# The last block of each chain behind the second product, transposes one block product later, last additions by halves

## The chip, the cores and the metric

One NeuronCore of a Trainium2 chip runs the whole program in one launch. The metric is the device time of one execution in microseconds (us). Engines by their short names: PE (matrix products, with PEld for its weight loads), DVE (vector), ACT (scalar), POOL (GpSimd), SP (which issues the DMAs). Each engine works through its own queue in order and waits on semaphores for the others.

## The reference

Local attention over 2304 tokens gives rows of 512 numbers; a first feed-forward block with ELU follows, then a mixture of eight experts whose weights `P` come from a softmax that is normalised by rows and columns eight times:

```python
for e in range(E):                       # 8 experts, F = 1024
    h = np.maximum(x @ w1[e], 0.0)       # x: 2304 x 512
    ye = h @ w2[e]
    out += P[:, e:e + 1] * ye
```

Everything is float32. The change touches only this last loop.

## The kernel before

Attention and the first block end at about 540 us, the softmax and five experts of the first 768 tokens at about 860 us. From there to the end runs the part that is changed. It takes the tokens in three groups of 768 (group 0 still lacks experts 5 to 7; groups 1 and 2 need all eight) and replaces each product of 2x2 blocks by seven block products (the scheme of Strassen and Winograd). Each float32 operand is held as a high and a low half, so one block product of 384 columns is 3 matmuls for each of two chunks of 128.

The work is cut into **periods**, one for each group, expert and half of the hidden units (6, 16 and 16 of them), and a period into seven **slots** `j`. A slot `s` issues, in program order:

- two block products of the first layer, by `l1` (6 matmuls each, into PSUM tiles `la` or `lb`). They belong to two **chains** `p` = 0 and 1. A chain takes its seven products `pi` in the order 1, 2, 6, 7, 5, 3, 4; chain 0 ends in slot 3, chain 1 in slot 6, each with product 4 into `lb`.
- one block product of the second layer, by `l2`, of the period eight slots earlier (`LAG`). For groups 1 and 2 that is `l2_flip`: 12 matmuls into a tile of two PSUM banks, `oa` and `ob` in turn, then one DVE addition of 768 columns into the sum `acc`. Column half `c` of the result lies in bank `c` of the tile.

Behind each `l1` stand operations that turn its PSUM result into the hidden blocks. ACT keeps copies (`a`, `u`, `v`, L1091); DVE adds them (`c`, L1085 and L1111), scales by `P` (L1081), and forms the sums of the scheme (`s`, L1095, with L1118 in front). Product 4 adds three: `c` <- `lb`, `u`; the scaling; a last `s`. Then `put` queues, in the list `after`, the split of each hidden block into halves: ACT copies the high half (L1044), DVE (L1049) or POOL (L1053) forms the low one. The list is emptied behind the next `l1` that isn't product 4.

At the end of a group the additions of the last four block products of `l2` (`done`, out of order 1, 7, 6, 4, 5, 2, 3) complete the four quarters of the result. Each is then added as two halves of 384 columns, both issued behind all 12 matmuls, and queues two `out_unit`s: three PE transposes into a tile `ot` of the ring `lb` (two buffers, shared with products 2, 7, 5 and 4 of the chains), an ACT copy to `ost`, and a DMA to the output. They are issued behind the `l2` of the next slot.

The order in each queue is the order in which this code calls the operations; no scheduler moves anything. Weights come by DMA, 12 tiles of `w1f` and 7 of `w2f` ahead.

Of the kernel before, what the change touches and what calls it, by code (L numbers as in the profile page):

```python
# [11 lines left out]
AF = mybir.ActivationFunctionType  # L12
ALU = mybir.AluOpType
# [5 lines left out]
def kernel(  # L19
# [14 lines left out]
    nc = tc.nc  # L34
# [645 lines left out]
    rest = others[N1 + N3:]  # L680
    for u in range(2 * KP):
        hs = [(4 * u + i, (4 * u + i) % 8) for i in range(4)]
# [176 lines left out]
    TH = 384  # L859
    NG2 = NT // (2 * TH)  # L860
# [81 lines left out]
    NPD = len(periods)  # L942
# [93 lines left out]

    chains = {}
    H = {}
    after = []

    def hid(key, slot, src, relu):
        h = P2["hp"].tile([P, 2, TH], R32, tag=f"h{slot}", bufs=3, name=f"h{slot}")
# [15 lines left out]
    def l1(k, n, p, pi):  # L1058
        key = (k, p)
        d = chains.setdefault(key, {})  # L1060
        if pi == 1:
            d["A"] = P2["ps2"].tile([P, 512], F32, tag="la", bufs=2, name="la")
        elif pi in (2, 7):
            d["B" if pi == 2 else "C"] = P2["ps2"].tile([P, 512], F32, tag="lb", bufs=2, name="lb")
        o = d["A" if pi in (1, 6, 5, 3) else "B" if pi == 2 else "C"][:, :TH]
        w, x = w1t.pop(n), xf[SLB[pi]]
        first = pi in (1, 2, 7)
        last = pi in (3, 2, 4)
        for c in range(2):
            for z, (a, b) in enumerate(((0, 0), (0, 1), (1, 0))):  # L1070
                nc.tensor.matmul(  # L1071
                    o, w[:, a, c, :], x[:, b, c, :],
                    start=first and c == 0 and z == 0, stop=last and c == 1 and z == 2,
                    skip_group_check=True,
                )

        g, e, _ = periods[k]

        def scaled(t, i):
            if g:  # L1080
                nc.vector.tensor_tensor(out=t, in0=t, in1=pb[g, e][:, i], op=ALU.mult)  # L1081

        def add(nm, a):
            t = tmp("c", 5, nm)
            nc.vector.tensor_tensor(out=t, in0=o, in1=d[a], op=ALU.add)  # L1085
            scaled(t, 0)
            d[nm] = t

        def keep(nm):
            d[nm] = tmp("a", 5, nm)  # L1090
            nc.scalar.activation(d[nm], o, AF.Copy)  # L1091

        def ssum(nm, a, b, op):
            d[nm] = tmp("s", 6, nm)
            nc.vector.scalar_tensor_tensor(d[nm], d[a], 0.0, d[b], op0=ALU.max, op1=op)  # L1095

        def put(slot, nm, relu):
            after.append(lambda: hid_low(*hid(key, slot, d[nm], relu)))

        if pi == 1:  # L1100
            keep("a")
        elif pi == 2:
            add("c11", "a")
            put(0, "c11", True)
        elif pi == 6:
            keep("u")
        elif pi == 5:
            keep("v")
            c = d["C"][:, :TH]
            t = tmp("c", 5, "c22")  # L1110
            nc.vector.tensor_tensor(out=t, in0=c, in1=d["v"], op=ALU.add)  # L1111
            scaled(t, 1)
            d["c22"] = t
            put(2, "c22", True)
        elif pi == 3:
            d["r21"] = tmp("s", 6, "r21")
            if g:
                nc.vector.scalar_tensor_tensor(  # L1118
                    d["r21"], o, 0.0, pb[g, e][:, 1], op0=ALU.max, op1=ALU.mult
                )  # L1120
            else:
                nc.scalar.activation(d["r21"], o, AF.Relu)
            ssum("s3", "c11", "r21", ALU.subtract)
            ssum("s1", "c22", "r21", ALU.add)
            ssum("s2", "c11", "s1", ALU.subtract)
            put(5, "s3", False)
            put(4, "s2", False)
            put(3, "s1", False)
        elif pi == 4:
            add("c21", "u")  # L1130
            ssum("s4", "c21", "s2", ALU.add)
            put(1, "c21", True)
            put(6, "s4", False)
            del chains[key]


    units = []

    def l2_flip(g, o, w, hs, fresh, i, j, init, done):
        acT = oa[g].rearrange("p a d -> p (a d)").rearrange("p (c t) -> p c t", c=NCC)  # L1140
        o = o.rearrange("p (c n) -> p c n", c=2)[:, :, :TH]
        for c in range(2):
            for p in range(2):
                for z, (a, b) in enumerate(((0, 0), (0, 1), (1, 0))):
                    nc.tensor.matmul(  # L1145
                        o[:, c],
                        w[:, p, b, c * P:(c + 1) * P],
                        hs[p][:, a, :],
                        start=fresh and p == 0 and z == 0,
                        stop=False,  # L1150
                        skip_group_check=True,
                    )
        ts = slice(i * TH, (i + 1) * TH)
        for cs in ((0, 1), (1, 2)) if done else ((0, 2),):
            a = acT[:, 2 * j + cs[0]:2 * j + cs[1], ts]
            src = o[:, cs[0]:cs[1]]
            if init:
                nc.scalar.activation(a, src, AF.Copy)
            else:
                nc.vector.tensor_tensor(out=a, in0=src, in1=a, op=ALU.add)  # L1160
        if done:
            units.append([lambda c=c: out_unit(g, acT, i, 2 * j + c) for c in range(2)])

# [16 lines left out]
    def l2(k, x):  # L1180
        g, e, pp = periods[k]
        pi = out_order[x]
        if x == 0:
            banks.reverse()
            ot["A"] = P2["ps2"].tile([P, 1024], F32, tag=banks[0], bufs=1, name=banks[0])
            if g == 2:
                oa[2] = oa[1]
            elif k and periods[k - 1][0] != g:
                oa[g] = accp.tile([P, 6, DM], F32, tag="acc2", name="acc2")
        if pi in (7, 2):  # L1190
            ot["B"] = P2["ps2"].tile([P, 1024], F32, tag=banks[1], bufs=1, name=banks[1])
        o = ot["A" if pi in (1, 6, 5, 3) else "B"]
        w = w2t.pop(7 * k + x)
        hs = [H.pop(((k, p), SLA[pi])) for p in range(2)]
        fresh = pi in (1, 7, 2)
        i, j, init = {
            1: (0, 0, True), 7: (1, 1, True), 6: (1, 0, True), 4: (1, 0, False),
            5: (1, 1, False), 2: (0, 0, False), 3: (0, 1, True),
        }[pi]
        last = pi in (2, 5, 4, 3)  # L1200
        done = last and e == E - 1 and pp == NP // 2 - 1
        if g:
            l2_flip(g, o, w, hs, fresh, i, j, init and e == 0 and pp == 0, done)
            return
        for c in range(3):
            for p in range(2):
                for z, (a, b) in enumerate(((0, 0), (0, 1), (1, 0))):
                    nc.tensor.matmul(  # L1208
                        o[:, c * HB2:(c + 1) * HB2],
                        hs[p][:, a, c * P:(c + 1) * P],  # L1210
                        w[:, p, b, :],
                        start=fresh and c != 1 and p == 0 and z == 0,
                        stop=False,
                        skip_group_check=True,
                    )
        for c in range(3):
            tt = 3 * i + c
            pe = Pr[:, g * 6 + tt, e:e + 1]
            a = oa[g][:, tt, j * HB2:(j + 1) * HB2]
            src = o[:, c * HB2:(c + 1) * HB2]  # L1220
            if init and e == 0 and pp == 0:
                nc.vector.tensor_scalar(a, src, pe, None, op0=ALU.mult)
            else:
                nc.vector.scalar_tensor_tensor(a, src, pe, a, op0=ALU.mult, op1=ALU.add)
        if done:
            t0 = (2 * g + i) * TH
            nc.sync.dma_start(
                out=out[t0:t0 + TH, j * HB2:(j + 1) * HB2].rearrange("(c p) d -> p c d", p=P),
                in_=oa[g][:, 3 * i:3 * i + 3, j * HB2:(j + 1) * HB2],
            )  # L1230


    with tc.manual_schedule():
# [6 lines left out]
            out=mask[:WIN], in_=mask[:WIN], compare_op=ALU.is_gt, fill=-1.0e9 / scale,  # L1240
# [4 lines left out]
            out=mask[:WIN], in_=mask[:WIN], compare_op=ALU.is_ge, fill=-1.0e9 / scale,  # L1245
# [50 lines left out]
        for m in range(NST + 3):  # L1296
# [58 lines left out]
            out=gw[:, :, E:2 * E], in0=gwr, in1=r(gw[:, :, 0:E]), op=ALU.subtract  # L1355
# [146 lines left out]
        for s in range(NPD * 7 + LAG):  # L1502
            k, j = divmod(s, 7)
            if k < NPD:
                for z, (p, pi) in enumerate(pairs[j]):
# [3 lines left out]
                    for f in fs:  # L1509
                        f()  # L1510
                    w1_load(s * 2 + z + NW1)
            while after and k >= NPD:
                after.pop(0)()
            fs = [f for u in units for f in u]
            units.clear()
            if s == LAG - 3:
                l2(0, 0)
            elif s > LAG:
                l2(*divmod(s - LAG, 7))
            for f in fs:  # L1520
                f()
            while nw2 <= min((s + 1) // 2 if s <= LAG else LAG // 2 + (s - LAG) * 3 // 2, s - LAG + NW2):
                w2_load(nw2)
                nw2 += 1
# [52 lines left out]
```

## Time and profile before

| what | value |
|---|---|
| time of three runs | 1990.64, 1994.05 and 1994.36 us, median 1994.05 |
| the profiled execution | 1989.62 us, of which its span is 1987.8 us |
| PE busy | 1968.5 us, 99% of the span |
| DVE, ACT, POOL busy | 73%, 43%, 37% of the span |
| PE's share of the chain that ended last | 91% (DVE 3%, ACT 2%, DMA 2%) |

PE is busy almost always, so an idle microsecond of PE is nearly a microsecond of the time. A busy share says nothing of who waits for whom; that is read from the waits and from the order of time. Times in the rows are us from the start of the span; a row of the timeline merges equal instructions that follow each other, and its bracket names the idle time before them with what ended it. A row of windows holds a stretch, its length, the busy time of PE, PEld, DVE, ACT and POOL (with the number of instructions), the granted clock of PE as a share of full speed, the share of the DMA engines and GB/s.

### The profile page before, as it was taken

The page shows a single profiled execution, that of the slowest core. Times are in us where ns is not written, and L with a number is a line of the kernel's source. Part 1 is how long each engine was busy: PE and PEld are TensorE (multiplying, and loading weights), DVE is VectorE, ACT ScalarE, POOL GpSimd, SP SyncE. Part 2 cuts the span into 40 slices and gives each one's busy share as a digit, 9 for nine tenths or more (in the row PEclk, how much of TensorE's full clock was granted, in tenths as well). Part 3 has the DMA queues.
Part 4 walks back from the last instruction along what each step waited for, and adds up shares of the span by engine and source line. Part 5 has one row for each costly group of instructions (what it writes and reads, how often), then busy time and mean ns, then how long its engine had stood idle before and what let it go on. Part 6 is the DMA issues. An engine that isn't in the chain of part 4 may idle for free.

```text
span 1987.8 us, 33576 instructions
## 1 busy us (share of the span) xinstructions
PE 1968.5 (99%) x11856; PEld 1826.8 (92%) x11856; DVE 1460.9 (73%) x2526; ACT 848.4 (43%) x1801; POOL 745.2 (37%) x725
## 2 busy tenths in 40 slices
PE   9999999999999999999999999999999999999998
PEld 7778888898878888899999999999998999999998
DVE  6745776767688666566787877887797877787786
ACT  8866455555443444343343333333334333333332
POOL 5423232333265555352262333323253323233232
PEclk9999999999999999999999999999999999999999
DMA  9751254457599999968878888888887888888883
GB/s 215 161 107 40 83 174 154 161 188 270 210 372 371 373 358 367 344 220 270 279 255 294 263 261 252 258 265 259 264 291 240 265 263 262 259 262 260 243 271 113
DMA packets 307718, 487.85 MB, mean 245 GB/s; under 512 B 79888, under 2 KB 162016, under 8 KB 303712
## 3 DMA queue, kind: packets, MB, share of 16 engines
q1 hardware_dynamic: 306288, 485.39, 76.0%
q8 instruction: 95, 1.56, 0.3%
q14 instruction: 71, 0.58, 0.1%
q10 hardware_dynamic: 1264, 0.33, 0.1%
HBM read 354.44 MB, written 126.95 MB: 242 GB/s over the span
## 4 chain that ended last, share of the span: by engine, by line
PE 91%; DVE 3%; ACT 2%; DMA 2%; issue 1%; SPq 0%; ACTq 0%; DVEq 0%
PE la L1071 16%; PE ob L1145 12%; PE oa L1145 11%; PE lb L1071 11%; PE p L879 3%; PE p L880 3%; PE p L881 3%; PE ac L897 3%; PE ac L898 3%; PE ac L899 3%; PE oa L1208 2%; PE ob L1208 2%; PE ac L531 2%; PE ac L532 2%; PE ac L533 2%; PE p L204 2%
## 5 line engine op out<-in xcount | busy, mean ns | idle before, releaser
L1053 POOL TENSOR_TENSOR h<-s,h 128x384 fp32r<-128x384 f32 x304 | 359.5, 1213 | 705.7 <-PE lb L1071 353.5
L1071 PE MATMUL la<-xf,w1f 128*128 128x384 f32 x1824 | 359.6, 335 | 0.7 <-ACT u L1091 0.7
L1071 PEld LDWEIGHTS la<-xf,w1f 128*128 128x128 f32 x1824 | 318.3, 188 | 1.4 <-ACT u L1091 1.3
L1071 PE MATMUL lb<-xf,w1f 128*128 128x384 f32 x1368 | 273.7, 334 | 0.0
L1145 PE MATMUL oa<-h,w2f 128*128 128x384 f32 x1344 | 251.3, 334 | 3.5 <-DVE acc L1160 3.5
L1145 PE MATMUL ob<-h,w2f 128*128 128x384 f32 x1344 | 251.2, 334 | 0.0
L1071 PEld LDWEIGHTS lb<-xf,w1f 128*128 128x128 f32 x1368 | 239.8, 188 | 0.0
L1145 PEld LDWEIGHTS oa<-h,w2f 128*128 128x128 f32 x1344 | 234.4, 188 | 4.2 <-DVE acc L1160 4.2
L1145 PEld LDWEIGHTS ob<-h,w2f 128*128 128x128 f32 x1344 | 234.4, 188 | 0.2
L1044 ACT ACTIVATE h<-s 128x384 fp32r<-128x384 f32 x304 | 146.7, 520 | 165.0 <-DVE s L1095 148.3
L1049 DVE SCALAR_TENSOR_TENSOR h<-c,h 128x384 fp32r<-128x384 f32 x228 | 161.5, 710 | 68.4 <-ACT h L1044 64.5
L718 POOL TENSOR_TENSOR sw<-rw 128x256 f32<-128x256 f32 x110 | 104.6, 951 | 202.9 <-DVE f L748 154.1
L1044 ACT ACTIVATE h<-c 128x384 fp32r<-128x384 f32 x228 | 119.1, 522 | 115.4 <-DVE c L1081 108.0
L1081 DVE TENSOR_TENSOR c<-c,pb 128x384 f32<-128x384 f32 x192 | 133.9, 698 | 6.6
L1160 DVE TENSOR_TENSOR acc<-oa,acc 128x768 f32<-128x768 f32 (+1 forms) x114 | 104.9, 923 | 28.9 <-PE oa L1145 28.9
L1160 DVE TENSOR_TENSOR acc<-ob,acc 128x768 f32<-128x768 f32 (+1 forms) x110 | 101.1, 923 | 28.3 <-PE ob L1145 28.3
L1095 DVE SCALAR_TENSOR_TENSOR s<-c,s 128x384 f32<-128x384 f32 x152 | 110.9, 730 | 13.8 <-DVE s L1095 0.5
L1091 ACT ACTIVATE a<-la 128x384 f32<-128x384 f32 x76 | 37.4, 492 | 191.2 <-PE la L1071 191.2
L246 ACT ACTIVATE hh<-p 128x512 fp32r<-128x512 f32 (+1 forms) x80 | 39.2, 491 | 186.0 <-PE p L881 186.0
L247 DVE SCALAR_TENSOR_TENSOR hl<-p,hh 128x512 fp32r<-128x512 f32 (+1 forms) x80 | 44.3, 556 | 90.1 <-ACT hh L246 90.1
L879 PE MATMUL p<-xh,f 128*128 128x512 f32 (+1 forms) x320 | 108.7, 340 | 0.0
L1091 ACT ACTIVATE v<-la 128x384 f32<-128x384 f32 x76 | 37.3, 491 | 165.9 <-PE la L1071 165.8
(172 smaller groups left out, 4077.6 us busy)
## 6 DMA issues: line engine op xcount, KB each, us to landing
w1f<-wdi SPq DMA_DIRECT2D x532, 256.0 KB, 4.0
w2f<-wdo SPq DMA_DIRECT2D x266, 512.0 KB, 4.3
wdo<-f SPq DMA_DIRECT2D x28, 1024.0 KB, 7.5
rw<-in_moe_w_dram SPq DMA_DIRECT2D x220, 128.0 KB, 5.1
wdi<-f SPq DMA_DIRECT2D x27, 1024.0 KB, 7.2
wdo<-f SPq DMA_DIRECT2D x28, 768.0 KB, 5.3
wdi<-f SPq DMA_DIRECT2D x27, 768.0 KB, 5.2
raw<-in_moe_w_in_dram SPq DMA_DIRECT2D x16, 512.0 KB, 4.2
```

Of the source, the lines that this page charges most:

```text
L718: nc.gpsimd.tensor_tensor(out=sw[:, o], in0=a, in1=b, op=op)
L879: nc.tensor.matmul(p1[:, :n], w[:, s, 0, cs], xh, start=(c == 0), stop=False)
L1044: nc.scalar.activation(h[:, 0], src, AF.Relu if relu else AF.Copy)
L1049: nc.vector.scalar_tensor_tensor(h[:, 1], src, 0.0, r(h[:, 0]), op0=ALU.max, op1=ALU.subtract)
L1053: nc.gpsimd.tensor_tensor(out=h[:, 1], in0=src, in1=r(h[:, 0]), op=ALU.subtract)
L1071: nc.tensor.matmul(o, w[:, a, c, :], x[:, b, c, :], start=first and c == 0 and z == 0, stop=last and c == 1 and z == 2, skip_group_check=True,
L1081: nc.vector.tensor_tensor(out=t, in0=t, in1=pb[g, e][:, i], op=ALU.mult)
L1091: nc.scalar.activation(d[nm], o, AF.Copy)
L1095: nc.vector.scalar_tensor_tensor(d[nm], d[a], 0.0, d[b], op0=ALU.max, op1=op)
L1145: nc.tensor.matmul(o[:, c], w[:, p, b, c * P:(c + 1) * P], hs[p][:, a, :], start=fresh and p == 0 and z == 0, stop=False, skip_group_check ...
L1160: nc.vector.tensor_tensor(out=a, in0=src, in1=a, op=ALU.add)
L1208: nc.tensor.matmul(o[:, c * HB2:(c + 1) * HB2], hs[p][:, a, c * P:(c + 1) * P], w[:, p, b, :], start=fresh and c != 1 and p == 0 and z == ...
```

## The change

Three edits. In `l1` the three DVE operations of product 4, with their two `put`s, go into a list `late`, which is emptied behind the slot's `l2`. In `l2_flip` a finished quarter's addition of half `c` is issued right behind that half's six matmuls, before the six of the other half. And the `out_unit`s are issued inside `l2_flip`, ahead of the additions that aren't last ones: in group 2 in the next slot as before, at the end of group 1 one slot later than before.

```diff
         elif pi == 4:
-            add("c21", "u")
-            ssum("s4", "c21", "s2", ALU.add)
-            put(1, "c21", True)
-            put(6, "s4", False)
+            def rest():
+                add("c21", "u")
+                ssum("s4", "c21", "s2", ALU.add)
+                put(1, "c21", True)
+                put(6, "s4", False)
+
+            late.append(rest)
             del chains[key]
...
-        for cs in ((0, 1), (1, 2)) if done else ((0, 2),):
-            a = acT[:, 2 * j + cs[0]:2 * j + cs[1], ts]
-            src = o[:, cs[0]:cs[1]]
-            if init:
-                nc.scalar.activation(a, src, AF.Copy)
-            else:
-                nc.vector.tensor_tensor(out=a, in0=src, in1=a, op=ALU.add)
+            if done:
+                a = acT[:, 2 * j + c, ts]
+                nc.vector.tensor_tensor(out=a, in0=o[:, c], in1=a, op=ALU.add)
+        if units and (g == NG2 - 1 and done or len(units) > 1 or x < 2):
+            for f in units.pop(0):
+                f()
+        if init:
+            nc.scalar.activation(acT[:, 2 * j:2 * j + 2, ts], o, AF.Copy)
+        elif not done:
+            a = acT[:, 2 * j:2 * j + 2, ts]
+            nc.vector.tensor_tensor(out=a, in0=o, in1=a, op=ALU.add)
...
-            while after and k >= NPD:
-                after.pop(0)()
-            fs = [f for u in units for f in u]
-            units.clear()
             if s == LAG - 3:
                 l2(0, 0)
             elif s > LAG:
                 l2(*divmod(s - LAG, 7))
-            for f in fs:
-                f()
+            while late:
+                late.pop(0)()
+            while after and k >= NPD:
+                after.pop(0)()
```

DVE's queue at the end of the last chain (slot 6 of the last period, and the next slot), before; L1160 is the addition of an `l2` into `acc`, L1085, L1081 and the last L1095 are product 4:

```order
L1095 SCALAR_TENSOR_TENSOR s_21543<-c_21454,s_21541 128x384 [waits DVE_49,Pool_49]
L1049 SCALAR_TENSOR_TENSOR h_21545<-c_21513,h_21545 128x384 [waits Activation_49]
L1085 TENSOR_TENSOR c_21554<-lb,u 128x384 [waits PE_49]
L1081 TENSOR_TENSOR c_21554<-c_21554,pb 128x384 [waits DVE_49]
L1095 SCALAR_TENSOR_TENSOR s_21557<-c_21554,s_21543 128x384 [waits DVE_49]
L1160 TENSOR_TENSOR acc_11683<-oa,acc_11683 128x2x384 [waits PE_49]
L1049 SCALAR_TENSOR_TENSOR h_21584<-c_21554,h_21584 128x384 [waits Activation_49]
L1160 TENSOR_TENSOR acc_11683<-ob,acc_11683 128x2x384 [waits PE_49]
```

The same place now (L1167 is the addition):

```order
L1095 SCALAR_TENSOR_TENSOR s_21543<-c_21454,s_21541 128x384 [waits DVE_49,Pool_49]
L1049 SCALAR_TENSOR_TENSOR h_21545<-c_21513,h_21545 128x384 [waits Activation_49]
L1167 TENSOR_TENSOR acc_11683<-oa,acc_11683 128x2x384 [waits PE_49]
L1085 TENSOR_TENSOR c_21568<-lb,u 128x384
L1081 TENSOR_TENSOR c_21568<-c_21568,pb 128x384 [waits DVE_49]
L1095 SCALAR_TENSOR_TENSOR s_21571<-c_21568,s_21543 128x384 [waits DVE_49]
L1167 TENSOR_TENSOR acc_11683<-ob,acc_11683 128x2x384 [waits PE_49]
L1049 SCALAR_TENSOR_TENSOR h_21597<-c_21568,h_21597 128x384 [waits Activation_49]
```

The addition from `oa` moved ahead of product 4's three operations, and the next one, from `ob`, ahead of a low half.

PE's queue in the last group, the first two block products whose additions are last ones (12 matmuls each into `ob`, then `oa`), before:

```order
L1145 MATMUL ob<-h_21388,w2f 128x384 [waits DMAHW5_49,DVE_49]
L1145 MATMUL ob<-h_21388,w2f 128x384 x2
L1145 MATMUL ob<-h_21545,w2f 128x384 x3
L1145 MATMUL ob<-h_21388,w2f 128x384 x3
L1145 MATMUL ob<-h_21545,w2f 128x384 x3
L1145 MATMUL oa<-h_21463,w2f 128x384 [waits DMAHW6_49,DVE_49]
L1145 MATMUL oa<-h_21463,w2f 128x384 x2
```

And now, on PE, the same two:

```order
L1149 MATMUL ob<-h_21388,w2f 128x384 [waits DMAHW5_49,DVE_49]
L1149 MATMUL ob<-h_21388,w2f 128x384 x2
L1149 MATMUL ob<-h_21545,w2f 128x384 x3
L1149 MATMUL ob<-h_21388,w2f 128x384 [waits DVE_49]
L1149 MATMUL ob<-h_21388,w2f 128x384 x2
L1149 MATMUL ob<-h_21545,w2f 128x384 x3
L1149 MATMUL oa<-h_21463,w2f 128x384 [waits DMAHW6_49]
L1149 MATMUL oa<-h_21463,w2f 128x384 x2
L1149 MATMUL oa<-h_21594,w2f 128x384 [waits Activation_49]
L1149 MATMUL oa<-h_21594,w2f 128x384
L1149 MATMUL oa<-h_21594,w2f 128x384 [waits Pool_49]
L1149 MATMUL oa<-h_21463,w2f 128x384 [waits DVE_49]
```

The order of these matmuls is as it was; a wait for DVE stands now in front of the seventh matmul of each product, and the one in front of the first of `oa` is gone.

DVE's queue at the end of group 1, from product 4 of chain 0 (slot 3) to the first addition by halves (slot 4), before:

```order
L1095 SCALAR_TENSOR_TENSOR s_16583<-c_16463,s_16581 128x384
L1085 TENSOR_TENSOR c_16593<-lb,u 128x384
L1081 TENSOR_TENSOR c_16593<-c_16593,pb 128x384
L1095 SCALAR_TENSOR_TENSOR s_16596<-c_16593,s_16583 128x384
L1160 TENSOR_TENSOR acc_11683<-oa,acc_11683 128x2x384
L1085 TENSOR_TENSOR c_16622<-lb,a 128x384
L1081 TENSOR_TENSOR c_16622<-c_16622,pb 128x384
L1049 SCALAR_TENSOR_TENSOR h_16634<-c_16593,h_16634 128x384
L1049 SCALAR_TENSOR_TENSOR h_16650<-c_16622,h_16650 128x384
L1160 TENSOR_TENSOR acc_11683<-ob,acc_11683 128x384 x2
```

And now:

```order
L1095 SCALAR_TENSOR_TENSOR s_16583<-c_16463,s_16581 128x384
L1167 TENSOR_TENSOR acc_11683<-oa,acc_11683 128x2x384
L1085 TENSOR_TENSOR c_16608<-lb,u 128x384
L1081 TENSOR_TENSOR c_16608<-c_16608,pb 128x384
L1095 SCALAR_TENSOR_TENSOR s_16611<-c_16608,s_16583 128x384
L1085 TENSOR_TENSOR c_16622<-lb,a 128x384
L1081 TENSOR_TENSOR c_16622<-c_16622,pb 128x384
L1049 SCALAR_TENSOR_TENSOR h_16634<-c_16608,h_16634 128x384
L1049 SCALAR_TENSOR_TENSOR h_16650<-c_16622,h_16650 128x384
L1159 TENSOR_TENSOR acc_11683<-ob,acc_11683 128x384 x2
```

Between the `s` and the halves stand the same eight operations in another order.

## Rows read from the trace of the kernel before

**Rows 1.** Windows: the two stretches of the changed part with idle PE.

```profile
1478.00:1537.00 59.00, 55.34 (x322) 53.80 (x322) 46.09 (x66) 25.19 (x50) 27.06 (x19) 1.00 0.78 235
...
1940.00:1988.00 48.00, 41.02 (x242) 39.97 (x240) 30.64 (x43) 11.96 (x25) 9.46 (x8) 0.99 0.38 110
```

**Rows 2.** PE's waits in 1072 to 1988 us: total, times, longest.

```profile
PE oa L1145 <- DVE acc L1160: 3.5, 2, 2.0
PE ot L1168 <- ACT ost L1170: 1.8, 3, 1.0
```

**Rows 3.** Timeline after the last chain: start us, duration us, instruction, idle before.

```profile
1961.55 0.55 DVE L1085 TENSOR_TENSOR c<-lb,u 128x384 f32<-128x384 f32 x1
...
1962.95 1.24 DVE L1095 SCALAR_TENSOR_TENSOR s<-c,s 128x384 f32<-128x384 f32 x1
...
1964.11 0.94 DVE L1160 TENSOR_TENSOR acc<-oa,acc 128x768 f32<-128x768 f32 x1
...
1965.11 2.38 PE L1145 MATMUL oa<-h,w2f 128*128 128x384 f32 x12 [1.96 <-DVE acc L1160]
...
1967.33 2.30 PE L1145 MATMUL ob<-h,w2f 128*128 128x384 f32 x12
```

**Rows 4.** Timeline, the other wait for an addition.

```profile
1491.46 0.54 DVE L1085 TENSOR_TENSOR c<-lb,u 128x384 f32<-128x384 f32 x1
...
1494.34 0.94 DVE L1160 TENSOR_TENSOR acc<-oa,acc 128x768 f32<-128x768 f32 x1
...
1498.60 0.94 DVE L1160 TENSOR_TENSOR acc<-ob,acc 128x768 f32<-128x768 f32 x1
...
1499.61 2.33 PE L1145 MATMUL ob<-h,w2f 128*128 128x384 f32 x12
```

**Rows 5.** Timeline at the end of group 1, slots 4, 5, 6 and 0.

```profile
1506.44 0.55 DVE L1085 TENSOR_TENSOR c<-lb,u 128x384 f32<-128x384 f32 x1
...
1508.03 2.24 PE L1145 MATMUL ob<-h,w2f 128*128 128x384 f32 x12
...
1512.18 2.24 PE L1145 MATMUL oa<-h,w2f 128*128 128x384 f32 x12
1512.44 1.01 DVE L1160 TENSOR_TENSOR acc<-ob,acc 128x384 f32<-128x384 f32 x2
1512.44 0.49 ACT L1091 ACTIVATE v<-la 128x384 f32<-128x384 f32 x1 [0.52 <-PE la L1071]
1513.37 0.55 DVE L1111 TENSOR_TENSOR c<-lb,v 128x384 f32<-128x384 f32 x1
...
1514.47 1.02 DVE L1160 TENSOR_TENSOR acc<-oa,acc 128x384 f32<-128x384 f32 x2
...
1517.88 2.25 PE L1145 MATMUL ob<-h,w2f 128*128 128x384 f32 x12
...
1519.85 0.55 DVE L1085 TENSOR_TENSOR c<-lb,u 128x384 f32<-128x384 f32 x1
...
1522.93 2.24 PE L1145 MATMUL oa<-h,w2f 128*128 128x384 f32 x12
...
1526.67 1.01 DVE L1160 TENSOR_TENSOR acc<-oa,acc 128x384 f32<-128x384 f32 x2
```

**Rows 6.** Windows around the longest idle PE of the trace: PE busy and PEclk.

```profile
554.00:557.00 3.00, 0.89 (x4) 0.47 (x3) 2.55 (x4) 2.23 (x4) 1.60 (x2) 1.00 1.03 432
557.00:561.00 4.00, 4.00 (x12) 2.39 (x12) 4.00 (x8) 1.06 (x1) 1.45 (x3) 0.57 1.06 376
```

**Rows 7.** Timeline of a slot 3 far from any group's end, and the slots behind it.

```profile
1713.38 2.24 PE L1145 MATMUL ob<-h,w2f 128*128 128x384 f32 x12
...
1714.81 0.55 DVE L1085 TENSOR_TENSOR c<-lb,u 128x384 f32<-128x384 f32 x1
...
1717.95 0.48 ACT L1091 ACTIVATE u<-la 128x384 f32<-128x384 f32 x1
...
1720.66 1.20 PE L1071 MATMUL la<-xf,w1f 128*128 128x384 f32 x6
```

More of the change, by code (lines that the diff above doesn't have):

```diff
@@ L1038 @@
     H = {}
-    after = []
+    after, late = [], []
     def hid(key, slot, src, relu):
@@ L1129, in l1, with l2_flip @@
         elif pi == 4:
-            add("c21", "u")
-            ssum("s4", "c21", "s2", ALU.add)
-            put(1, "c21", True)
-            put(6, "s4", False)
+            def rest():
[4 more added lines that the diff above has]
+            late.append(rest)
             del chains[key]
     units = []
-    def l2_flip(g, o, w, hs, fresh, i, j, init, done):
+    def l2_flip(x, g, o, w, hs, fresh, i, j, init, done):
         acT = oa[g].rearrange("p a d -> p (a d)").rearrange("p (c t) -> p c t", c=NCC)
         o = o.rearrange("p (c n) -> p c n", c=2)[:, :, :TH]
+        ts = slice(i * TH, (i + 1) * TH)
         for c in range(2):
@@ L1152, in l2_flip @@
                     )
-        ts = slice(i * TH, (i + 1) * TH)
-        for cs in ((0, 1), (1, 2)) if done else ((0, 2),):
-            a = acT[:, 2 * j + cs[0]:2 * j + cs[1], ts]
-            src = o[:, cs[0]:cs[1]]
-            if init:
-                nc.scalar.activation(a, src, AF.Copy)
-            else:
-                nc.vector.tensor_tensor(out=a, in0=src, in1=a, op=ALU.add)
+            if done:
[9 more added lines that the diff above has]
+            nc.vector.tensor_tensor(out=a, in0=o, in1=a, op=ALU.add)
         if done:
@@ L1202, in l2 @@
         if g:
-            l2_flip(g, o, w, hs, fresh, i, j, init and e == 0 and pp == 0, done)
+            l2_flip(x, g, o, w, hs, fresh, i, j, init and e == 0 and pp == 0, done)
             return
```

## The prediction

> **What bounds the kernel now.** I read the page's busy shares first, then the windows of the changed part, then PE's waits in it, and only then the timeline around each wait. The busy shares say PE, 99%. The windows say where the missing per cent of the changed part lies: in the stretch 1478 to 1537, at the end of group 1, PE is idle for 59.00 - 55.34 = 3.7 us, and in the last 48 us for 48.00 - 41.02 = 7.0 us, part of it behind PE's last instruction [rows 1]. PE's waits name the causes: two waits for an addition into `acc`, 3.5 us together, and three waits of a transpose for the copy to `ost`, 1.8 us [rows 2]. So at most some 6 us can be won here, and everything else that the change does must be judged by whether it makes PE wait anew.
>
> PE's pace is the unit of what follows. An `l2` of 12 matmuls starts 2.08 us before whatever follows it, its first six take 1.04 us, and the row shows 2.24 because the last matmul is still draining (0.16 more). After a wait it takes 2.22 instead (1965.11 to 1967.33 [rows 3]), so each new wait also costs a restart of 0.14.
>
> **Product 4 behind the second product.** After the last chain PE stands 1.96 us before `oa` and is free again at 1965.11, because DVE does product 4's three operations (from 1961.55) before the addition that PE needs [rows 3]. With the addition first it starts at 1961.55 and is over by 1962.5, and PE, idle since 1965.11 - 1.96 = 1963.15 and able to start 0.16 before that, at 1962.99, doesn't wait. But the three operations now stand before the next addition, from `ob`: they take 1964.11 - 1961.55 = 2.56 us, from 1962.42 to 1964.98; the addition ends at 1965.92. PE, with 2.08 us for `oa` from 1962.99, is at `ob` by 1965.07 and waits until 1965.98, against 1967.33 before: 1.35 us won. The last `s` takes 1.24 with POOL at work beside it, and a little later POOL may be done; at the 0.55 of the `c` in front of it 2.0 us are won. I take **-1.6**, between the two.
>
> The other wait, near 1495, gains nothing. DVE runs without a gap there: the addition from `oa` moves from 1494.34 to 1491.46, yet the same eight operations still end with the addition from `ob` at 1498.60 + 0.94, and PE needs exactly that one at 1499.61 [rows 4]. What PE wins before `oa` it waits before `ob`. Bounds: 1.6 won if DVE finishes earlier, 0.5 lost if the late `c` holds `lb`; I take **0**.
>
> In the steady part the addition from `lb` now waits for `l2`'s end, so product 4's results come later. In a quiet slot 3 DVE would begin `c` at 1713.38 + 2.24 + 0.04 + 0.94 = 1716.6 instead of 1714.81, 1.8 us later; ACT's copy `u`, queued behind the copy of the last `s`, moves from 1717.95 to 1719.75 and ends at 1720.23, and PE overwrites its source at 1720.66 [rows 7]. That is 0.4 us of cover, so **0**, and the thinnest cover of the change.
>
> **Last additions by halves.** The second half's six matmuls write the other bank of the tile, and one would think that they run while DVE adds the first half. The program as built says otherwise: a wait for DVE stands before the seventh matmul, and it is for the addition of the first half of the same tile, since the next product, into `oa`, needs no wait any more for an addition that comes earlier in DVE's queue. The tile is guarded as a whole. So PE stops in the middle of each of the eight last products (four at the end of group 1, four in group 2) until DVE has added 384 columns.
>
> The Trainium skill ("PSUM — Partial Sum Buffer", section "PSUM bank collisions raise a hardware error") says that a matmul's write and a vector read clash in one bank and run clean in different banks. By that the wait isn't needed; it would give the third rival's time. No run so far has such a pair, but the wait is in the program, and PE obeys it.
>
> The price with an idle DVE: the sixth matmul ends 1.20 us after the start, DVE starts 0.04 later, half an addition takes 0.55 and PE starts 0.06 after it (1964.11 + 0.94 to 1965.11 [rows 3]). That is 1.85 instead of 1.04: 0.81, with the restart 0.95. In group 2 DVE is idle there, four times: **+3.8**.
>
> At the end of group 1 the addition stands behind other work in DVE's queue, and there PE's queue is not ahead but waits. Four products, each by what DVE did before [rows 5]; an addition that starts at A frees PE at A + 0.55 + 0.06:
>
> - Slot 4: `l2` starts at 1508.03, its seventh matmul would at 1509.07. DVE's eight operations from 1506.44 on are the same in either order, so the half starts at 1512.44 as before. PE resumes at 1513.05: 3.98 late.
> - Slot 5: DVE needs `v`, which starts 0.26 behind `l2` (1512.18 to 1512.44) and takes 0.49, with 0.04 to DVE's start, then `c` and its scaling, 1514.47 - 1513.37 = 1.10. The half starts 1.89 behind the start of `l2`: 1.89 + 0.61 - 1.04 = 1.46.
> - Slot 6: it stands where the `c` of 1519.85 stood, 1.97 behind the start of `l2` at 1517.88: 1.54.
> - Slot 0: at 1526.67, 3.74 behind the start at 1522.93: 3.31.
>
> Together 10.3, with four restarts **+10.8**. Before, DVE came late in the same slots but nothing asked for its result for another slot; that was the cover, and it is gone.
>
> **The clock.** A wait of 4 us may also cost PE its clock. The longest idle PE of the trace, 2.1 us in 554 to 557, was followed by 4 us at a granted 0.57 of full speed, most of it at the lower of the two levels (1.2 of 2.4 GHz); that loses 4 x 0.43 = 1.7 us [rows 6]. The idle 1.96 us at 1963 lost nothing. So I count one fall, behind the wait of slot 4: **+1.7**.
>
> The Trainium skill ("TensorE: Matmul & The Clock Gate", section "HAM oscillation — how this bites in real kernels") says that PE falls back to its low clock in idle gaps and that a loop with such a gap in every turn pays each time. By that the wait of slot 0 pays as well, 1.7 us more than the row that I go by; the range holds it.
>
> **Transposes.** At the end of group 1 they move one slot, with two ACT copies and two output DMAs each; on SP the stores pass a few weight loads, whose tiles are 7 and 12 ahead, some 20 us. Three of the four pairs find one buffer of the `lb` ring, as two or three do now, so the 1.8 us [rows 2] stay about as they are: **0**, within 1 either way. In group 2 their place on PE is the same, and behind the last product the end hangs on copies and buffers, not on the addition: **0**.
>
> **Sum.** -1.6 + 0 + 3.8 + 10.8 + 1.7 = +14.7 us on the profiled execution's 1989.62, which gives 2004.3. The median of the runs is 4.4 above that execution, so I forecast 1994.05 + 14.7, or 2008.7.
>
> **Rivals.**
>
> 1. *The bare price.* If DVE isn't behind at the end of group 1 (PE's first waits give it time to catch up), all eight stops cost 0.95: 7.6 - 1.6 = +6.0, 2000. For it: each wait of PE is time for DVE. Against: in slots 5, 6 and 0 the additions follow what PE itself has just finished, so waiting doesn't help.
> 2. *A late `u`.* If the cover of 0.4 us [rows 7] is gone in practice, `la` waits in slot 5 of each of the 32 periods of groups 1 and 2. Each 0.2 us that is missing costs 6.4; with 0.2, 2015. Against: in the quiet period of the rows nothing waits for `u` even after the move.
> 3. *Not slower.* If the seventh matmul's wait is met already when PE comes to it (it is for an older addition), the halves run beside PE, as the edit means them to. Then only -1.6 is left, up to -3.2 with the wait of 1495: 1991 to 1992.5. It decides at one place, the wait before the seventh matmul; the order of the waits speaks against it.
>
> **Chances.** Forecast 0.72, bare price 0.12, late `u` 0.10, not slower 0.06. What a measurement of this kernel can tell from no change is about 0.2%, 4 us. Forecast, bare price and late `u` lie beyond that (a bare price with a kind DVE may not); the third rival lies within it but for its best end. So slower 0.92, same 0.06, faster 0.02. The range runs from below the bare price by the 3.4 us between the lowest run and the median, 1997, to the forecast with a second fall of the clock and a little of the late `u`, 2016.
>
> **What would show it.** Right: a new PE wait, the line of the second product (L1149) for the addition by halves (L1159), eight times, some 13 us, the longest about 4 us; PE's wait before the first `l2` behind the last chain gone or under 1 us and moved from `oa` to `ob`; granted clock under 1.00 near 1515. Wrong: no such wait, or waits of 0.8 us all eight times, or waits of `la` for `u` all over the steady part.

## The result, and the profile after

The changed kernel takes 2006.76 us (median of six runs, 2005.06 to 2010.37), beside 1994.2 of the kernel before in the same comparison: 1.007 times as long, interval 1.006 to 1.008, or 12 to 16 us more. It is slower. One of the six runs of the kernel before took 3690.8 us; it is left out of the ratio and moves that median by 0.15. The forecast of 2008.7 is 1.9 above the median; the range and the sign held. The profiled execution took 2006.37 us (span 2004.4) against 1989.62 before, +16.75, where the sum said +14.7.

Windows of the two stretches of [rows 1], after (columns as there):

```profile
1478.00:1550.00 72.00, 59.79 (x330) 56.81 (x328) 49.42 (x70) 26.12 (x52) 29.74 (x22) 0.98 0.64 197
...
1950.00:2005.00 55.00, 46.72 (x268) 44.36 (x267) 33.95 (x48) 13.38 (x28) 12.72 (x12) 0.99 0.39 113
```

At the end of group 1 PE is idle for 72.00 - 59.79 = 12.2 us, where it was idle for 3.7. PE's waits from 1072 us to the end, which answer to [rows 2] (us in total, times, longest):

```profile
PE ob L1149 <- DVE acc L1159: 6.5, 4, 3.9
PE oa L1149 <- DVE acc L1159: 5.7, 4, 3.2
PE ot L1175 <- ACT ost L1177: 2.2, 4, 0.6
PE lb L1071 <- DVE c L1085: 1.0, 1, 1.0
PE la L1071 <- ACT u L1091: 0.9, 2, 0.7
PE lb L1071 <- DVE c L1111: 0.7, 1, 0.7
PE ob L1149 <- DVE acc L1167: 0.2, 1, 0.2
```

The first two rows are the new wait: the second product for the addition by halves, eight times, 12.2 us. The two waits of `oa` for a whole addition (3.5 us before) are gone; 0.2 before `ob` is left, in the last row. The rows between, of `lb` and `la` for product 4's `c` (L1085), for `u` and for the `c` made with `v` (L1111), are new too. The forecast's sum has them at 0; it names a late `c` that holds `lb` as a bound, and a late `u` as its second rival.

The order of time where the answer lies, the end of group 1 (start, duration, instruction, idle before):

```profile
1510.61 1.20 PE L1149 MATMUL ob<-h,w2f 128*128 128x384 f32 x6
...
1513.41 1.82 DVE L1049 SCALAR_TENSOR_TENSOR h<-c,h 128x384 fp32r<-128x384 f32 x2
1515.15 0.54 DVE L1159 TENSOR_TENSOR acc<-ob,acc 128x384 f32<-128x384 f32 x1
1515.75 2.21 PE L1149 MATMUL ob<-h,w2f 128*128 128x384 f32 x6 [3.93 <-DVE acc L1159]
1517.76 1.91 PE L1071 MATMUL lb<-xf,w1f 128*128 128x384 f32 x6
1519.50 1.20 PE L1071 MATMUL la<-xf,w1f 128*128 128x384 f32 x6
1520.54 1.21 PE L1149 MATMUL oa<-h,w2f 128*128 128x384 f32 x6
1523.00 1.32 PE L1149 MATMUL oa<-h,w2f 128*128 128x384 f32 x6 [1.25 <-DVE acc L1159]
...
1526.24 1.21 PE L1149 MATMUL ob<-h,w2f 128*128 128x384 f32 x6
1528.74 1.33 PE L1149 MATMUL ob<-h,w2f 128*128 128x384 f32 x6 [1.30 <-DVE acc L1159]
...
1533.53 1.20 PE L1149 MATMUL oa<-h,w2f 128*128 128x384 f32 x6
1537.90 1.33 PE L1149 MATMUL oa<-h,w2f 128*128 128x384 f32 x6 [3.17 <-DVE acc L1159]
```

Each product that was one row of 12 in [rows 5] is now two rows of 6 with a wait between. How late the seventh matmul is comes from the starts (the bracket is 0.16 or 0.17 less, since it counts from the drained end): 1515.75 - 1510.61 - 1.04 = 4.10, then 1.42, 1.46 and 3.33. The forecast had 3.98, 1.46, 1.54 and 3.31. Behind the first stop the next six matmuls take 2.01 instead of 1.16 (1.04 and 0.12 of restart), the six after them 1.74 instead of 1.04: 1.55 us are lost to the clock. The windows show it (the last three columns: PEclk, DMA share, GB/s):

```profile
1515.00:1518.00 3.00, 2.25 (x7) 2.25 (x8) 0.70 (x3) 0.00 (x0) 0.00 (x0) 0.64 0.00 0
1518.00:1521.00 3.00, 3.00 (x15) 3.00 (x15) 0.55 (x1) 0.20 (x1) 0.00 (x0) 0.79 0.63 175
...
1538.00:1541.00 3.00, 3.00 (x20) 2.96 (x21) 0.56 (x1) 1.41 (x4) 1.01 (x1) 1.00 0.00 0
```

Behind the 3.93 the granted clock is 0.64 and 0.79 of full speed, behind the 3.17 it is 1.00.

The end of the last chain, which answers to [rows 3], and the first stop in group 2:

```profile
1974.48 3.58 POOL L1053 TENSOR_TENSOR h<-s,h 128x384 fp32r<-128x384 f32 x3 [6.22 <-ACT h L1044]
...
1976.13 0.94 DVE L1167 TENSOR_TENSOR acc<-oa,acc 128x768 f32<-128x768 f32 x1
1977.00 0.54 DVE L1085 TENSOR_TENSOR c<-lb,u 128x384 f32<-128x384 f32 x1
1977.56 2.25 PE L1149 MATMUL oa<-h,w2f 128*128 128x384 f32 x12
...
1978.51 0.56 DVE L1095 SCALAR_TENSOR_TENSOR s<-c,s 128x384 f32<-128x384 f32 x1
...
1979.99 2.38 PE L1149 MATMUL ob<-h,w2f 128*128 128x384 f32 x12 [0.18 <-DVE acc L1167]
...
1984.34 1.20 PE L1149 MATMUL ob<-h,w2f 128*128 128x384 f32 x6
...
1986.21 1.31 PE L1149 MATMUL ob<-h,w2f 128*128 128x384 f32 x6 [0.67 <-DVE acc L1159]
```

The addition from `oa` is ahead of product 4, PE doesn't wait before `oa`, and the last `s` takes 0.56 here instead of 1.24; POOL's work is over (at 1978.06) when it starts. In group 2 the seventh matmul is 1986.21 - 1984.34 - 1.04 = 0.83 late; in the other three products it is 0.81, 0.91 and 0.92 late.

To see where the time went, I take the start of the first matmul of the first layer in each period (numbered 0 to 37), and subtract the same start in the trace of before; the last row compares the ends of PE's last instruction. The columns are the changed kernel and the eight experiments below, in their order:

```
period (before)   after    1     2     3     4     5     6     7     8
20   (1429.12)    0.42   0.23  2.96 -0.16  3.81  3.19  2.27  2.92 -0.05
22   (1487.36)    2.75   2.20  3.90  1.32  5.35  4.78  4.22  3.57  1.13
24   (1553.22)   14.58   2.38 19.42  2.41  5.55  4.98 14.45  3.58  1.44
37   (1931.78)   14.58   2.38 19.42  2.41  5.54  4.98 14.45  3.58  1.44
end  (1983.24)   16.53   0.60 23.17  0.59  3.35  6.92 16.46  1.78 -0.73
```

What stands in the first row comes, but for 0.6 at most, from stages ahead of the changed part and from one execution each; only the steps between rows are read. One source of it can be named: near 503 us PE was idle for 2.78 to 2.91 us in experiments 2, 4, 5, 6 and 7, and their granted clock in 505 to 508 was 0.50 to 0.70; in the other five executions, before among them, it was idle for 1.20 to 2.01 us and the clock stayed at 1.00. For the changed kernel: +2.33 in 1429 to 1487, +11.83 at the end of group 1, exactly 0 through thirteen periods, +1.95 at the end. The last splits into 1979.99 - 1967.33 - 14.58 = -1.92 behind the last chain, and +3.87 for group 2's four stops (3.47 of lateness and four restarts).

### The profile page after: what moved, and what is told of

The parts are those of the page before. It is cut to its first block, busy times and chain, and to the rows that moved or that the text cites. A ratio compares the mean times of both kernels' runs of the same rounds, so it can differ in the third digit from the quotient of the medians.

```text
span 2004.4 us, 33519 instructions
## 1 busy us (share of the span) xinstructions
PE 1974.3 (98%) x11856; PEld 1828.7 (91%) x11856; DVE 1476.4 (74%) x2526; ACT 845.5 (42%) x1801; POOL 742.4 (37%) x725
## 3 DMA queue, kind: packets, MB, share of 16 engines
q8 instruction: 95, 1.56, 0.3%
## 4 chain that ended last, share of the span: by engine, by line
PE 87%; DVE 6%; ACT 3%; DMA 2%; issue 1%; SPq 1%; POOL 0%; DVEq 0%; ACTq 0%; POOLq 0%
PE la L1071 15%; PE lb L1071 11%; PE ob L1149 11%; PE oa L1149 10%; PE p L879 3%; PE p L881 3%; PE p L880 3%; PE ac L898 3%; PE ac L897 3%; PE ac L899 3%; PE oa L1215 2%; PE ob L1215 2%; PE ac L531 2%; PE ac L533 2%; PE ac L532 2%; PE p L204 2%
## 5 line engine op out<-in xcount | busy, mean ns | idle before, releaser
L1149 PE MATMUL ob<-h,w2f 128*128 128x384 f32 x1344 | 253.2, 335 | 6.7 <-DVE acc L1159 6.5
L1149 PE MATMUL oa<-h,w2f 128*128 128x384 f32 x1344 | 252.3, 335 | 5.7 <-DVE acc L1159 5.7
L1149 PEld LDWEIGHTS ob<-h,w2f 128*128 128x128 f32 x1344 | 235.0, 188 | 8.3 <-DVE acc L1159 7.8
L1149 PEld LDWEIGHTS oa<-h,w2f 128*128 128x128 f32 x1344 | 234.3, 188 | 7.1 <-DVE acc L1159 7.0
L1049 DVE SCALAR_TENSOR_TENSOR h<-c,h 128x384 fp32r<-128x384 f32 x228 | 186.0, 827 | 54.8 <-ACT h L1044 52.4
L1081 DVE TENSOR_TENSOR c<-c,pb 128x384 f32<-128x384 f32 x192 | 130.9, 682 | 6.6
L1167 DVE TENSOR_TENSOR acc<-oa,acc 128x768 f32<-128x768 f32 x106 | 101.0, 953 | 33.9 <-PE oa L1149 33.9
L1167 DVE TENSOR_TENSOR acc<-ob,acc 128x768 f32<-128x768 f32 x102 | 97.2, 953 | 33.8 <-PE ob L1149 33.8
L880 PE MATMUL p<-xl,f 128*128 128x512 f32 (+1 forms) x320 | 107.6, 336 | 0.0
```

Of the source, the lines that this page charges most:

```text
L880: nc.tensor.matmul(p1[:, :n], w[:, s, 0, cs], xl, start=False, stop=False)
L1049: nc.vector.scalar_tensor_tensor(h[:, 1], src, 0.0, r(h[:, 0]), op0=ALU.max, op1=ALU.subtract)
L1149: nc.tensor.matmul(o[:, c], w[:, p, b, c * P:(c + 1) * P], hs[p][:, a, :], start=fresh and p == 0 and z == 0, stop=False, skip_group_check ...
L1167: nc.vector.tensor_tensor(out=a, in0=o, in1=a, op=ALU.add)
```

## The experiments

Two theories stood against each other: that the stop between the halves is the loss, each as long as DVE is behind at its place (the forecast's), and that the late product 4 is, by filling DVE's queue or by holding `la` and `lb`. Differences in us are the ratio's distance from 1 times the median of before in the same rounds (1992.66 for experiments 1 to 4, 1993.24 for 5 to 8), and the brackets are 95% intervals. Theories and rivals in the quoted expectations are those of each experiment.

A difference of 1 or 2 us can be one of the clock. The granted clock is listed for every run, to 0.001 of full speed: it averages 0.9984 and 0.9982 for the kernel before in the two sets of rounds, and 0.9986 to 0.9991 for experiments 1, 3, 4, 5, 7 and 8. At 2 us for each thousandth that is, as an estimate, 0.9 to 1.4 us in favour of these six. All six lack PE's wait of 1.96 us behind the last chain [rows 3], but whether other executions of before lose their clock there is not shown; the profiled one did not.

**1. Last additions whole again.** The changed kernel with

```diff
-            if done:
-                a = acT[:, 2 * j + c, ts]
-                nc.vector.tensor_tensor(out=a, in0=o[:, c], in1=a, op=ALU.add)
+        for c in range(2 if done else 0):
+            a = acT[:, 2 * j + c, ts]
+            nc.vector.tensor_tensor(out=a, in0=o[:, c], in1=a, op=ALU.add)
```

> The changed kernel with one edit undone: a finished quarter's two additions stand behind all 12 matmuls again, product 4 late and the transposes moved stay. Theory A (the stop between the halves is the loss): PE's waits of L1149 for an addition in the middle of a product vanish, with them the 3.9 of group 2 and most of the 11.8 at the end of group 1; what is left is the +2.3 of the stretch 1429 to 1487 and the -1.9 at the end of the last chain, so 0 to +1 us against before. Rival B (the late product 4 or the moved transposes make DVE late at the end of group 1): 8 to 12 us of the 12.7 stay.

Measured: 1990.67 us, ratio 0.9991 (0.9982 to 1.0), or -1.8 us (-3.6 to 0). In the trace +1.97, +0.18 and -1.78 in the three places, +0.37 together. PE's waits:

```profile
PE lb L1071 <- DVE c L1085: 1.0, 1, 1.0
PE la L1071 <- ACT u L1091: 0.7, 1, 0.7
...
PE ob L1149 <- DVE acc L1167: 0.2, 1, 0.2
```

No wait of L1149 for a half is left, and the loss at the end of group 1 is gone with it: theory A. By the time it is a little faster than expected. Some 1.4 us of that go with the clock, by the estimate above; and the expectation was read against an execution of before that lost nothing in 1429 to 1487 and took 4.4 us less than the median of its runs.

**2. Halves only.** The kernel before, with the last addition of each half right behind its six matmuls:

```diff
+            if done:
+                a = acT[:, 2 * j + c, i * TH:(i + 1) * TH]
+                nc.vector.tensor_tensor(out=a, in0=o[:, c], in1=a, op=ALU.add)
...
-        for cs in ((0, 1), (1, 2)) if done else ((0, 2),):
+        for cs in () if done else ((0, 2),):
```

> The kernel before with one edit alone: each half's last addition right behind its six matmuls. Theory A: the stops cost here what they cost in the changed kernel, 11.8 + 3.9, so +15 to +16 us against before, with the longest wait near 4 us and a fall of the granted clock behind it. Rival B (the stops are dear only because the late product 4 fills DVE's queue at the end of group 1): the bare price of 0.95 for each of eight, +8 us or less.

Measured: 2012.93 us, ratio 1.0095 (1.0081 to 1.0109), or +18.9 (16.1 to 21.7). The halves alone make the loss, so rival B falls; but it is 3 us more than expected. The trace gives +3.75 for group 2, as expected, and +15.52 at the end of group 1 instead of 11.8. Two things make that. The stop of slot 6 is more than twice as long (PE and DVE, start, duration):

```profile
1529.93 1.21 PE L1145 MATMUL ob<-h,w2f 128*128 128x384 f32 x6
...
1531.89 0.55 DVE L1085 TENSOR_TENSOR c<-lb,u 128x384 f32<-128x384 f32 x1
...
1533.55 0.55 DVE L1155 TENSOR_TENSOR acc<-ob,acc 128x384 f32<-128x384 f32 x1
...
1534.15 1.33 PE L1145 MATMUL ob<-h,w2f 128*128 128x384 f32 x6 [3.02 <-DVE acc L1155]
```

Product 4 of chain 1 stands ahead of the half and takes 1533.55 - 1531.89 = 1.66; in the changed kernel it is late, and the stop is 1.30. So with halves in place the late product 4 wins 1.7 us there. And the clock falls twice: 2.5 us are lost behind a stop of 3.77, 1.6 behind one of 3.11 (from the starts of the products behind each, as above).

**3. Late product 4 only.** The kernel before, with

```diff
-            add("c21", "u")
-            ssum("s4", "c21", "s2", ALU.add)
-            put(1, "c21", True)
-            put(6, "s4", False)
+            def rest():
+                add("c21", "u")
+                ssum("s4", "c21", "s2", ALU.add)
+                put(1, "c21", True)
+                put(6, "s4", False)
+
+            late.append(rest)
```

and the list emptied behind the slot's `l2`.

> The kernel before with one edit alone: product 4's three operations and its two splits behind the slot's second product. Theory A: -1.9 at the end of the last chain and +2.3 in the stretch 1429 to 1487 (PE waits for c and u there), nothing in the other periods: 0 to +1 us against before. Rival B (it makes the loss at the end of group 1): +8 us or more. Rival C (late u holds la in the steady part): +6 us or more, spread evenly over the periods.

Measured: 1993.26 us, ratio 1.0001 (0.9992 to 1.001), or +0.2 (-1.6 to +2.0). In the trace +1.48, +1.09, 0 through the steady periods, -1.82 at the end: theory A, and rivals B and C fall. The 1.09 at the end of group 1 has 1.8 us of transposes that wait for a `c` in their ring; with the transposes moved (experiment 1) those are 0.6, and the step is 0.18. So the moved transposes are worth some 0.9 beside a late product 4.

**4. Two tiles of one bank.** The changed kernel with the guarded unit made smaller:

```diff
-            ot["A"] = P2["ps2"].tile([P, 1024], F32, tag=banks[0], bufs=1, name=banks[0])
+            ot["A"] = [P2["ps2"].tile([P, 512], F32, tag=f"{banks[0]}{c}", bufs=1, name=banks[0]) for c in range(2)]
...
-        if init:
-            nc.scalar.activation(acT[:, 2 * j:2 * j + 2, ts], o, AF.Copy)
-        elif not done:
-            a = acT[:, 2 * j:2 * j + 2, ts]
-            nc.vector.tensor_tensor(out=a, in0=o, in1=a, op=ALU.add)
+        for c in range(0 if done else 2):
+            a = acT[:, 2 * j + c, ts]
+            if init:
+                nc.scalar.activation(a, o[c][:, :TH], AF.Copy)
+            else:
+                nc.vector.tensor_tensor(out=a, in0=o[c][:, :TH], in1=a, op=ALU.add)
```

> The changed kernel with each tile of two PSUM banks made of two tiles of one bank; all additions and first copies into acc go by halves of 384 columns. The seventh matmul of a last product then waits for no addition of its own first half. Theory A (the guard on the whole tile is what stops PE): the eight stops vanish, 0 to +2 us against before. Rival B (a DVE read of one bank beside PE's writes to the other stops PE itself, or the split additions of all other products cost DVE so much that PE waits): +10 us or more.

Measured: 1991.05 us, ratio 0.9994 (0.9985 to 1.0003), or -1.2 (-3.0 to +0.6). The matmuls and the last additions by halves are those of the changed kernel. The tile is another, and so that it can be, all other additions and the first copies go by halves too, which adds to DVE's work. PE's waits from 1072 us on have none for an addition any more: the eight stops are gone. The last products of group 2, where a half is added while PE goes on:

```profile
1974.90 2.24 PE L1148 MATMUL ob<-h,w2f 128*128 128x384 f32 x12
...
1976.13 0.56 DVE L1158 TENSOR_TENSOR acc<-ob,acc 128x384 f32<-128x384 f32 x1 [0.48 <-PE ob L1148]
1976.98 2.25 PE L1148 MATMUL oa<-h,w2f 128*128 128x384 f32 x12
```

DVE reads the first bank from 1976.13 to 1976.69, in the middle of PE's matmuls into the second, and PE's 12 take the usual 2.08 from start to start. So the rule that the forecast weighed (the Trainium skill, "PSUM — Partial Sum Buffer", section "PSUM bank collisions raise a hardware error": a write and a read in different banks run clean) agrees with this run. It was the tile's guard, not the memory, that stopped PE.

**5. Halves in group 2 only.** The changed kernel, group 1's last additions behind all 12 matmuls:

```diff
-            if done:
+            for h in (c,) if g == 2 else (0, 1) if c else ():
+                if done:
```

> The changed kernel, but the last additions of group 1 stand behind all 12 matmuls; those of group 2 go by halves. Theory A (each stop costs what DVE is behind at its place): group 2's four stops cost 0.95 to 0.97 each, 3.9 together, nothing is lost at the end of group 1, so +4 to +5 us against before, 3.9 above the kernel with all last additions whole. Rival B (half of the loss is paid for any stop, wherever): group 2's four cost half of the 15.7, +8 us against before.

Measured: 1995.64 us, ratio 1.001 (1.0001 to 1.0019), or +2.0 (0.2 to 3.8); in the trace +1.59, +0.20 and +1.94, where the last is 3.7 above experiment 1's -1.78. Rival B's +8 is out: a stop costs what DVE is behind at its place. Against before the time is below the expected 4 to 5, as in experiment 1; 3.8 above that one, by the ratios of two sets of rounds, it is as expected.

**6. The first stop taken out.** The changed kernel, with only slot 4's last addition of group 1 whole:

```diff
-            if done:
+            for h in (c,) if g == 2 or x != 3 else (0, 1) if c else ():
+                if done:
```

> The changed kernel, but the first last product of group 1 (slot 4, whose stop was 3.93 us) has its two halves behind all 12 matmuls. Theory A (a stop is local: the 3.93 and the fall of the clock behind it belong to this place): from the order of time of the kernel with whole last additions, DVE gets to the half of slot 5 at 1516.59, PE then waits some 2.0 there instead of 1.25, and the later stops are as before; the clock stays. That wins 3.9 + 0.1 + 1.7 - 0.7 = 5.0: about +7.7 us against before (6 to 9.5). Rival B (DVE's backlog goes on: slot 5 waits as much more as slot 4 waits less, and the clock falls there): +11 us or more.

Measured: 2003.21 us, ratio 1.0053 (1.004 to 1.0066), or +10.6 (8.0 to 13.2): neither theory's number. The stops behaved as theory A said, the clock didn't (PE, start, duration, idle before):

```profile
1519.24 1.33 PE L1149 MATMUL oa<-h,w2f 128*128 128x384 f32 x6 [1.82 <-DVE acc L1160]
1520.41 2.00 PE L1071 MATMUL la<-xf,w1f 128*128 128x384 f32 x6
1522.20 2.01 PE L1071 MATMUL lb<-xf,w1f 128*128 128x384 f32 x6
1524.05 1.22 PE L1149 MATMUL ob<-h,w2f 128*128 128x384 f32 x6
...
1535.06 2.29 PE L1149 MATMUL oa<-h,w2f 128*128 128x384 f32 x6 [3.17 <-DVE acc L1160]
1537.15 1.48 PE L1176 MATMUL ot<-ident,acc 128*128 128x128 f32 x6
1538.29 2.27 PE L1071 MATMUL la<-xf,w1f 128*128 128x384 f32 x6
1540.35 1.53 PE L1071 MATMUL lb<-xf,w1f 128*128 128x384 f32 x6
```

The seventh matmul of slot 5 is 1.98 late (2.0 expected), slot 6's 0.83 (1.46 in the changed kernel), slot 0's 3.33: 6.14 instead of 10.31, so DVE's backlog does not go on. But the clock falls behind the 1.82 (1.56 us lost, by the starts) and again behind the 3.17 (2.74 lost):

```profile
1520.00:1523.00 3.00, 3.00 (x13) 3.00 (x12) 1.04 (x2) 0.00 (x0) 0.00 (x0) 0.59 0.48 112
...
1535.00:1538.00 3.00, 2.94 (x11) 2.84 (x11) 0.57 (x2) 0.52 (x1) 0.90 (x1) 0.50 0.02 8
1538.00:1541.00 3.00, 3.00 (x12) 3.00 (x12) 0.00 (x0) 1.39 (x4) 0.09 (x1) 0.50 0.48 131
```

That is 4.30 against 1.55. The stops' -4.17 and the clock's +2.75 leave -1.4, and the step between the rows 22 and 24 is 10.23 instead of 11.83, -1.6. Not every execution falls twice: the profiled one (2006.27) and one of 2006.46 us have a granted clock of 0.996, the other three (2001.96 to 2003.21) 0.998 or 0.999. These three are 8.7 to 10.0 us above the median of before, at and just above the upper end of theory A's 6 to 9.5.

**7. Late product 4 at the end only.** Experiment 3, with

```diff
-            late.append(rest)
+            late.append(rest) if k >= 24 else rest()
```

> The kernel before with one edit alone, and only from the third period of group 2 on: product 4 behind the slot's second product. Theory A (the +2.3 of the stretch 1429 to 1487 comes from late product 4 beside the planning of group 2's operands, and late product 4 is free in quiet periods): PE as before up to 1932, 1.8 to 1.9 won behind the last chain: -1.9 us against before. Rival B (the +2.3 is another run's chance, or comes with any late product 4): +0.4 us.

Measured: 1990.69 us, ratio 0.9981 (0.9972 to 0.999), or -3.8 (-5.6 to -2.0). It is the only version whose whole interval lies below the kernel before, so by the time it beats both kernels. In the trace PE keeps its pace up to period 37 but for 0.65 in 1429 to 1487, and behind the last chain 1.80 are won, -1.15 together:

```profile
1966.56 2.24 PE L1148 MATMUL oa<-h,w2f 128*128 128x384 f32 x12
...
1968.98 2.38 PE L1148 MATMUL ob<-h,w2f 128*128 128x384 f32 x12 [0.18 <-DVE acc L1163]
```

The time's interval ends at -2.0, beyond what the trace shows. Some 1.4 us go with the clock (0.9989 on average, 0.9982 for before); the gain that rows of this trace show is 1.2 to 1.8. The 0.65 stands where this kernel's instructions are those of before, and so does experiment 2's 0.94. Of the +2.33 of the changed kernel a part is therefore chance from one execution to the next: 0 to 0.94 without the late product 4 (before, experiments 2 and 7), 1.48 to 2.33 with it (the changed kernel and experiments 1 and 3 to 6).

**8. Both.** Experiment 4 with the late product 4 of experiment 7:

> Tiles of one bank with all last additions by halves, moved transposes, and product 4 late only from the third period of group 2 on: what the runs so far point to. Theory A: no stop in the middle of a product, nothing lost in the stretch 1429 to 1487, some 2 us won at the end (the halves give 0.4 more than whole additions): -1.5 to -2.5 us against before. Rival B (additions by halves, 16% more DVE time for each, make DVE late where it plans group 2's operands): 0 to +3 us.

Measured: 1992.7 us, ratio 0.9993 (0.9983 to 1.0002), or -1.4 (-3.4 to +0.4); in the trace +1.18, +0.31 and -2.17. The end is 0.4 better than in experiment 7, as expected. In 1429 to 1487 it loses 0.5 more than experiment 7, but that is less than what executions differ by there, so rival B is not decided. The time can't tell it from before. Experiment 7 has the lowest ratio of all, though its interval overlaps those of experiments 1, 4 and 8.

## Why the prediction was right

**The stops.** The step that carried the forecast, that the tile is guarded as a whole, is shown by experiment 4 from one side and by 1 and 2 from the other. The sizes were read from the trace of before by asking when DVE would come to the half: 10.29 us of lateness forecast at the end of group 1, 10.31 measured; +3.8 for group 2, 3.87 measured. The bare price (rival 1) failed for the reason given: in slots 5, 6 and 0 the half stands behind work that follows what PE has just finished. The largest stop, in slot 4, stands behind the eight operations that DVE still has to do.

**The end of group 1 as a whole.** Forecast +10.8 and +1.7 for the clock; measured +11.83. The lateness and four restarts of 0.12 make 10.8, the clock 1.55; together 12.3. The 0.5 less that was measured lies in two other places, by the starts: the transposes there lose 3.0 us instead of 3.4 (their waits are 0.64, 0.50 and 0.95 long before, and three times 0.64 now), and the place near 1495 loses 1.8 instead of 1.9.

**Product 4 at the end.** Forecast -1.6 between 1.35 and 2.0; measured -1.92. POOL was done by the last `s` (0.56, not 1.24), so the upper end was the nearer one. The mechanism was as described; the wait that was to move to `ob` is there, 0.18 long.

**The wait near 1495.** Forecast 0, and nearly 0 came out (1.8 us lost there instead of 1.9, and +0.18 for the whole end of group 1 in experiment 1), but in another way than told. PE does not wait before `ob`; it waits a little earlier, because the late `c` and a late `u` hold `lb` and `la` (the last two rows; the forecast had the held `lb` as a bound only):

```profile
1442.82 0.56 DVE L974 TENSOR_TENSOR xt<-xb,xb 128x384 f32<-128x384 f32 x1 [3.80 <-DMA xb<-x2d]
...
1443.90 1.31 PE L1071 MATMUL lb<-xf,w1f 128*128 128x384 f32 x6 [0.67 <-DVE c L1111]
...
1453.19 1.32 PE L1071 MATMUL la<-xf,w1f 128*128 128x384 f32 x6 [0.70 <-ACT u L1091]
...
1496.52 1.31 PE L1071 MATMUL lb<-xf,w1f 128*128 128x384 f32 x6 [1.04 <-DVE c L1085]
...
1500.08 2.37 PE L1071 MATMUL la<-xf,w1f 128*128 128x384 f32 x12 [0.17 <-ACT u L1091]
```

**The missed term.** The rows from 1442.82 to 1453.19 show what failed: "That is 0.4 us of cover, so 0" was read from one quiet slot and taken for all. In quiet periods it holds exactly (0.00 through periods 24 to 37, so rival 2 was rightly small). In 1429 to 1487, where DVE and POOL also plan group 2's operands (L974 on DVE), the cover is gone: `la` waits 0.70 for `u` at 1453.19, which costs 0.96 from start to start, and 0.33 more are lost at 1485.82. All six kernels with a late product 4 there show both, 1.3 us together; the kernel before and experiments 2 and 7 show neither, and experiment 8, whose other additions go by halves, loses 0.45 at the second place alone. The wait at 1443.90 is another: DVE has stood idle for 3.80 us, for the DMA of a planned operand, just ahead of the `c` that PE waits for. It costs 0 to 0.94 in these executions, and experiment 2 has it (0.44) without a late product 4. That the planning is what takes the cover away is argued from the place and from these rows; no run moves it. So the edit as such was worth nothing: -1.9 at one end, 1.5 to 2.3 lost at the other, of which 1.3 are its own; only where experiment 7 confines it is it a gain.

**The clock.** One fall of 1.7 was forecast, one of 1.55 seen in this profile. That was partly luck: the profiled executions of experiments 2 and 6, with long stops at the same end of group 1, fell twice, and the profiled execution of the changed kernel has the highest granted clock of its six runs (0.999; the others 0.997 or 0.998). The sum of +14.7 stands beside 16.1 in the trace from 1429 us on and 12 to 16 by the ratio; the missed 2.33 is the largest error of the sum, and the range was wide enough for it.

## What to carry to other kernels

Before splitting an operation to overlap its halves with the producer, look what the halves are guarded by: in this program the wait belonged to the tile, so the overlap needed one tile for each half, not only one bank. The price of such a stop is how far the consumer is behind at that place, read from its queue in the order of time, and not the length of the half. A cover read in a quiet period must be read again in the busiest one; an edit that pays at one place is often best confined to it.

## What was not expected of the hardware

How long PE was idle did not decide whether the granted clock fell. At the end of group 1 it fell with idle times of 3.93 and 1.82 us (1.55 and 1.56 us lost), and of 3.77 and 3.11 (2.5 and 1.6). With 3.17 it stayed at 1.00 in the changed kernel and fell to 0.50 for 6 us in experiment 6 (2.74 lost); with 3.02 in experiment 2, and with 1.96 behind the last chain in the kernel before, nothing was lost. The Trainium skill ("TensorE: Matmul & The Clock Gate", "HAM oscillation — how this bites in real kernels") describes a loop in which PE waits some 3 to 5 us for a DMA in every turn and starts every turn at its low clock. Of the six stops over 3 us named here four agree and two don't, and the one of 1.82 fell although it is shorter. What tells them apart stays open: no run varied it alone. With each fall worth 1.5 to 2.7 us, and with executions of one kernel (experiment 6) that differ in it, this is an uncertainty that a forecast of a stop of a few us has to carry.
